# Relu-squared attention and a gated feed-forward product on one core: another order of the same 735 steps

## The chip, the cores and the metric

The kernel runs on one core of a Trainium2 chip. The metric is the time of one execution on the device in microseconds (us). Times are medians of several executions. A run that is more than 1.5% above the fastest of the same kernel counts as slow and is left out. The span in a profile is the time of the one execution that was profiled, and is about 2 us shorter than the time on the clock of the same run.

TensorE is called PE in the profile (its weight loads PEld), VectorE DVE, ScalarE ACT, GpSimd POOL, SyncE SP.

## The reference

```python
# q, k, v: (8 batches, 12 heads, 448 tokens, 64) float32
scores = np.matmul(q, k.transpose(0, 1, 3, 2)) / 8.0
attn   = np.maximum(scores, 0.0) ** 2 / 448
x      = np.matmul(attn, v).transpose(0, 2, 1, 3).reshape(3584, 768)
h      = x @ w_in                                  # w_in  (768, 2048)
g      = h * (1.0 / (1.0 + np.exp(-1.702 * h)))
out    = g @ w_out                                 # w_out (2048, 768), result float32
```

## The kernel before

The work is cut into 24 units (a batch by four heads). For each unit, the kernel loads q, k and v, brings q and k into transposed form, computes seven blocks of scores, relus, squares them, and multiplies by v. The first six units are loaded with a cast and transposed on TensorE; later ones are loaded by Sync, cast by ScalarE and GpSimd, and transposed by DMA. The token blocks of x are gathered in eight groups; each group passes through the two feed-forward products.

Nothing is scheduled by a tool: the order of all instructions is one list of short words that a loop reads. Each engine executes its instructions in the order of that list.

```python
        zp = ps_m.tile([128, 512], F32, name="zp", tag="mm")
        for _ in range(8):
            nc.tensor.matmul(out=zp, lhsT=zero[:, 0:128], rhs=zero[:, 0:512], start=True, stop=True)
        # ... cut ...
        def slot(how, u, j):                        # "s": one block of scores, then its relu
            sc = scores(u, j, 2 if "t" in how else 1)
            if "h" in how:                          # ":h": relu held until the next f step
                held.append((u, j, sc))
            else:
                ats[u, j] = relu2(u, j, sc, "d" in how)   # ":d": relu on VectorE, else ScalarE

        def zeros(how, n):                          # "z": n matmuls of zeros into a scores bank
            early.append(ps_s.tile([128, 2, 512], F32, name="sc", tag="sc"))
            for _ in range(n):
                nc.tensor.matmul(out=early[0][:, 0, :], lhsT=zero[:, 0:128],
                                 rhs=zero[:, 0:512], start=True, stop=True)

        do = {"s": slot, "x": square, "z": zeros,
              "k": lambda how, u: trans_pe(u, "k"), "q": lambda how, u: trans_pe(u, "q"),
              # ... cut: a, b attention x v; f first product; m, p, i second product ...
              "jk": lambda how, u: load16(u, "k"), "jq": lambda how, u: load16(u, "q"),
              "jv": lambda how, u: load_v(u), "jw": lambda how, i: w1(i),
              "jo": lambda how, h, i: w2(h, i), "I": lambda how: make_identity(nc, ident),
              # ... cut: G gate; L, W later loads; K, Q casts; R transposes by DMA ...
```

The zero matmuls compute nothing that is used: they only keep TensorE active while the first loads are on their way. The loads `jk`, `jq`, `jv` (of k, q, v), `jw` (w_in), `jo` (w_out) and the making of the identity `I` are all issued by GpSimd, in listed order. And the buffers of q and k have three places each, so a fourth `jq` has to wait until the first q was transposed.

## Time and profile before

| | before |
|---|---|
| median (lowest to highest) of 4 runs | 389.35 us (389.01 to 389.63) |
| span of the profiled execution | 388.4 us |
| TensorE busy | 370.6 us of it |
| lost on TensorE in the first 24 us | 8.8 us |
| lost later | 8.6 us, 2.4 of it on one wait for w_out |

The profiled execution was at the upper end (390.16 us on the clock), so that differences between traces come out up to 0.8 us smaller than those between medians.

The two lines below are from TensorE's instructions in order of time, before: start, duration, the operation and its tiles, and the count of instructions in the row.

```profile
4.61 1.16 PE L466 MATMUL sc<-zero 128*128 128x512 f16 x3
5.70 0.58 PE L129 MATMUL tr<-ident,q 128*64 128x128 f16 x14
```

The old order lists the step `z3` first. TensorE is active from 1.22 us until the first transpose at 5.70. The second view is of busy time in stretches (columns: stretch, its length, then busy time of PE, PEld, DVE, ACT, POOL with the number of instructions, the granted clock, the share of the DMA rings and GB/s).

```profile
5.30:8.70 3.40, 2.34 (x62) 1.43 (x60) 1.81 (x3) 0.37 (x1) 3.40 (x6) 1.00 1.21 178
8.70:12.10 3.40, 1.87 (x50) 1.38 (x50) 2.98 (x6) 2.27 (x3) 2.10 (x4) 1.00 1.20 180
```

TensorE waits for loads here, but it still works 2.34 and 1.87 of 3.40 us.

### The profile page before, as it was taken

Reading aid. Unit: us, or ns where it says so; the run is one execution under the profiler, and the core shown is the slowest. Engines: PE = TensorE matmul, PEld = TensorE weight load, DVE = VectorE, ACT = ScalarE, POOL = GpSimd, SP = SyncE. Lnnn points to the kernel's source line nnn. Section 1 sums busy time; section 2 is a strip of 40 time slices with the busy share of each in tenths; the row PEclk is TensorE's granted clock in tenths of the full one; section 3 lists DMA queues with packets and bytes.
Section 4 is the critical chain, followed back from the end, with each engine's and each line's share of the span. In section 5 each row is a group of like instructions: output and inputs, shape, how many; then the busy total and the mean of one; then the engine's idle time right before and its main releaser. Section 6 shows DMA issues by size and latency. Waiting matters only on the chain.

```text
span 388.4 us, 8391 instructions
## 1 busy us (share of the span) xinstructions
PE 370.6 (95%) x3390; PEld 195.4 (50%) x3390; DVE 262.4 (68%) x433; ACT 218.4 (56%) x320; POOL 136.8 (35%) x200
## 2 busy tenths in 40 slices
PE   7699999799999999999999999999999999999994
PEld 3566654344444545454455455555455555545552
DVE  3889774689977987846767777377965845114474
ACT  2796855578748546566865948446934452242210
POOL 8537417516443213344451244212234132232100
PEclk9999999999999999999999999999999999999999
DMA  8999999999750769899774194643140600210323
GB/s 117 199 203 182 204 259 198 233 216 176 207 138 2 145 168 193 183 230 207 181 173 133 41 154 102 154 99 110 25 106 0 130 1 17 66 42 1 83 81 82
DMA packets 65223, 50.88 MB, mean 131 GB/s; under 512 B 35744, under 2 KB 61728, under 8 KB 65184
## 3 DMA queue, kind: packets, MB, share of 16 engines
q1 hardware_dynamic: 47872, 35.70, 37.7%
q0 software_dynamic: 17152, 14.55, 25.8%
q8 instruction: 26, 0.43, 0.4%
q10 hardware_dynamic: 160, 0.10, 0.1%
q14 instruction: 13, 0.11, 0.1%
HBM read 45.61 MB, written 11.01 MB: 146 GB/s over the span
## 4 chain that ended last, share of the span: by engine, by line
PE 79%; DVE 9%; DMA 6%; issue 3%; POOL 2%; ACT 1%; ACTq 0%; POOLq 0%
PE ht L245 34%; PE op L310 27%; PE sc L166 8%; PE av L197 6%; DVE at L453 4%; DMA wout<-in_moe_w_out_dram 4%; DMA v<-in_v_dram 2%; PE op L271 2%; DVE osb L321 2%; DVE rl L177 1%; PE tr L129 1%; PE avm L197 1%; DVE xt L220 1%; ACT rl L180 1%; POOL k L119 1%
## 5 line engine op out<-in xcount | busy, mean ns | idle before, releaser
L245 PE MATMUL ht<-xt,win 128*128 128x512 f16 (+2 forms) x768 | 157.9, 353 | 0.2 <-ACT ea L319 0.2
L252 POOL TENSOR_SCALAR gt<-gf 128x512 f16<-128x512 f32 (+2 forms) x128 | 82.6, 645 | 214.0 <-ACT gf L250 212.4
L180 ACT ACTIVATE rl<-sc 128x896 f16<-128x896 f32 x148 | 130.1, 922 | 45.3 <-PE sc L166 37.0
L453 DVE TENSOR_TENSOR at<-rl 128x896 f16<-128x896 f16 x168 | 109.1, 681 | 17.8 <-ACT rl L180 17.4
L250 ACT ACTIVATE gf<-ht 128x512 f32<-128x512 f32 (+2 forms) x128 | 69.7, 548 | 87.8 <-PE ht L245 75.2
L245 PEld LDWEIGHTS <-win 128*128 128x128 f16 x768 | 72.1, 98 | 74.0 <-issue 11.6
L310 PEld LDWEIGHTS <-gt 128*128 128x128 f16 x424 | 40.5, 98 | 31.1 <-issue 4.5
L166 PE MATMUL sc<-qT,kT 64*64 64x448 f16 (+4 forms) x816 | 48.2, 324 | 2.3 <-ACT rl L180 1.5
L310 PEld LDWEIGHTS <-as 128*128 128x128 f16 x320 | 30.4, 98 | 24.3 <-issue 3.6
L310 PE MATMUL op<-wout,as 128*128 128x384 f16 x224 | 40.4, 326 | 0.0
L310 PE MATMUL op<-wsum,gt 128*128 128x384 f16 x224 | 40.2, 326 | 0.0
L217 DVE CAST xt<-av 128x768 f16<-128x768 f32 (+5 forms) x34 | 24.1, 735 | 20.4 <-PE av L197 20.4
L321 DVE SCALAR_TENSOR_TENSOR osb<-op,osb 128x384 f32<-128x384 f32 (+1 forms) x49 | 25.7, 545 | 15.4 <-PE op L310 15.2
L310 PE MATMUL op<-wout,gt 128*128 128x384 f16 (+1 forms) x200 | 35.3, 320 | 0.8 <-DVE osb L321 0.8
L197 PE MATMUL av<-at,v 64*64 64x448 f16 (+3 forms) x668 | 33.1, 331 | 1.2 <-DVE at L453 0.6
L166 PEld LDWEIGHTS <-kT 64*64 64x64 f16 x816 | 19.2, 105 | 25.2 <-issue 18.2
L305 DVE TENSOR_TENSOR as<-gt 128x1024 f16<-128x1024 f16 x38 | 27.6, 752 | 3.4 <-POOL gt L252 3.4
L321 DVE SCALAR_TENSOR_TENSOR osb<-op,ea 128x384 f32<-128x384 f32 x24 | 13.2, 551 | 24.4 <-ACT eb L319 12.6
L197 PEld LDWEIGHTS <-v 64*64 64x64 f16 x816 | 21.5, 107 | 16.3 <-issue 7.0
L177 DVE TENSOR_SCALAR rl<-sc 128x896 f16<-128x896 f32 x20 | 21.7, 1086 | 6.5 <-PE sc L166 6.4
L104 POOL CAST q<-qst 128x896 f16<-128x896 f32 x18 | 17.8, 987 | 6.3 <-DMA qst<-in_q_dram 5.5
L91 POOL DMA_DIRECT2D v<-in_v_dram x24 | 18.1, 757 | 1.0
(38 smaller groups left out, 167.4 us busy)
## 6 DMA issues: line engine op xcount, KB each, us to landing
out_dram<-osb SPq DMA_DIRECT2D x54, 192.0 KB, 3.0
kst<-in_k_dram SPq DMA_DIRECT2D x18, 448.0 KB, 5.4
qst<-in_q_dram SPq DMA_DIRECT2D x18, 448.0 KB, 5.8
v<-in_v_dram POOLq DMA_DIRECT2D x24, 224.0 KB, 6.2
win<-in_moe_w_in_dram POOLq DMA_DIRECT2D x8, 384.0 KB, 9.5
wout<-in_moe_w_out_dram POOLq DMA_DIRECT2D x4, 768.0 KB, 12.5
q<-in_q_dram POOLq DMA_DIRECT2D x6, 224.0 KB, 7.4
k<-in_k_dram POOLq DMA_DIRECT2D x6, 224.0 KB, 8.6
```

The lines of the kernel that those rows point to most:

```text
L166: nc.tensor.matmul(out=sc[c, a, c0:c0 + 64 * (q1 - q0)], lhsT=st["kT"][r, kb, c], rhs=st["qT"][r, q0:q1, c], start=True, stop=True)
L177: nc.vector.tensor_scalar(out=rl, in0=sc[:, :, 0:S], scalar1=0.0, scalar2=None, op0=ALU.max)
L180: nc.scalar.activation(out=rl, in_=sc[:, :, 0:S], func=AF.Relu)
L197: nc.tensor.matmul(out=st["av"][s][64 * a:64 * a + 64, 64 * (q0 - base):64 * (q1 - base)], lhsT=st["v16"][r, a, 64 * kb:64 * kb + 64], rhs ...
L217: nc.vector.tensor_copy(out=xts[g][:, 2 * pr:2 * pr + 2, c], in_=st["pair"][:, :, f])
L245: nc.tensor.matmul(out=ht[:, 0:n], lhsT=w[:, kk, fo:fo + 128], rhs=xts[g][:, kk, 0:n], start=(kk == 0), stop=(kk == NK - 1))
L250: nc.scalar.activation(out=gf[:, 0:n], in_=ht[:, 0:n], func=AF.Gelu_apprx_sigmoid, scale=1.0 / SC)
L252: nc.gpsimd.tensor_scalar(out=gts[g][:, f, 0:n], in0=gf[:, 0:n], scalar1=SC, scalar2=1.0, op0=ALU.mult, op1=ALU.mult)
L305: nc.vector.tensor_tensor(out=out_, in0=x, in1=y, op=op)
L310: nc.tensor.matmul(out=op[:, 0:cw], lhsT=lhs[:, f, :], rhs=w[:, f, c0:c0 + cw], start=(start and f == 0), stop=(stop and f == HF - 1))
L321: nc.vector.scalar_tensor_tensor(out=o, in0=op[:, 0:w], scalar=sc, in1=add, op0=ALU.mult, op1=ALU.add)
L453: nc.vector.tensor_tensor(out=at, in0=rl, in1=rl, op=ALU.mult)
```

## The change

The list of words is replaced by another one. The multiset of steps is the same but for the marks `:d`, `:h` and `:m`. The new list is meant to share the DMA rings better between the engines that issue transfers, and to place loads, casts and transposes of batch 2 and later well ahead of their use. It also gives VectorE 31 relus in place of 20. The core of the diff, with cuts:

```diff
         words = (
-            "z3 jq0 jk0 I jk1 q0 jq2 k0 s0.0:d x0.0 jq1 s0.1 jk2 s0.2 q2 x0.1 jv1 k1 jv0 s0.3 "
+            "jk0 I k0 jq0 q0 s0.0 jk1 s0.1 s0.2:d k1 jq1 x0.0 jk2 z3 q1 jq2 k2 s1.0 x0.1 jq5 "
 # ... cut ...
-            "s5.2 x5.1 s5.3 a4:m s5.4 x5.2 x5.3 x5.4 s5.5 s5.6:d x5.6 K6 K7 x5.5 m0.1.0 a5 "
-            "m0.0.0 f1.0 jo1.1 jo1.0 f1.1 f1.2 Q7 R6 f1.3 s6.0 L8 C1 s6.1:d K8 R7 C3 x6.1 Q8 W6 "
+            "s4.5 x4.3 x4.5 x4.4 s4.6 f0.12 f0.13 x4.6 s5.0 s5.1 x5.0 a4 jo1.0 s5.2:h f0.14 "
+            "f0.15 s5.3 x5.1 s5.4:d x5.2 s5.5 x5.3 x5.4 s5.6 x5.5 L7 C0 m0.1.0 x5.6 K6 Q6 R6 Q7 "
+            "C2 a5 jo1.1 m0.0.0 f1.0 L8 f1.1 f1.2 C3 C1 f1.3 f1.4 f1.5 s6.0 s6.1:d s6.2 x6.0 "
+            "x6.1 K7 f1.6 x6.2 s6.3 s6.4:d R7 x6.3 E2 B3 f1.7 f1.8 K8 Q8 f1.9 f1.10 W6 R8 s6.5 "
 # ... cut: all later lines are re-ordered in the same way ...
```

## The prediction

> **What bounds the kernel now.** I read the page first (busy shares, chain), then PE's waits, then PE's instructions in order of time, then busy time in 10 us stretches.
>
> ```profile
> PE 370.6 (95%) x3390; PEld 195.4 (50%) x3390; DVE 262.4 (68%) x433; ACT 218.4 (56%) x320; POOL 136.8 (35%) x200
> PEclk9999999999999999999999999999999999999999
> ...
> PE 79%; DVE 9%; DMA 6%; issue 3%; POOL 2%; ACT 1%; ACTq 0%; POOLq 0%
> ```
>
> TensorE is the bound: 370.6 of 388.4 us busy at full clock, 79% of the chain. So a new order can only gain what PE waits. Where that is:
>
> ```profile
> 7.70 0.78 PE L166 MATMUL sc<-qT,kT 64*64 64x256 f16 x32 [0.72 <-DVE kT L133]
> 9.21 0.58 PE L129 MATMUL tr<-ident,q 128*64 128x128 f16 x14 [0.74 <-DMA q<-in_q_dram]
> 11.29 0.58 PE L129 MATMUL tr<-ident,q 128*64 128x128 f16 x14 [0.79 <-DMA q<-in_q_dram]
> 12.38 0.58 PE L129 MATMUL tr<-ident,k 128*64 128x128 f16 x14 [0.51 <-DMA k<-in_k_dram]
> 14.30 0.39 PE L166 MATMUL sc<-qT,kT 64*64 64x256 f16 x8 [0.63 <-ACT rl L180]
> 15.19 0.97 PE L197 MATMUL avm<-at,v 64*64 64x256 f16 x40 [0.50 <-DMA v<-in_v_dram]
> 18.61 0.39 PE L197 MATMUL avm<-at,v 64*64 64x192 f16 x8 [0.68 <-DVE at L453]
> ...
> 75.45 2.77 PE L271 MATMUL op<-wout,gt 128*128 128x384 f16 x16 [2.43 <-DMA wout<-in_moe_w_out_dram]
> ```
>
> The start waits for loads, then for relu on ACT and squares on DVE; at 75 us the first right-half output product waits 2.43 us for a wout quarter. The stretches, columns PE, PEld, DVE, ACT, POOL busy, show who is full then:
>
> ```profile
> 10.00:20.00 10.00, 6.59 (x236) 5.07 (x231) 8.31 (x17) 7.63 (x10) 5.38 (x8) 1.00 1.24 199
> 20.00:30.00 10.00, 9.36 (x233) 6.34 (x227) 8.82 (x18) 9.10 (x14) 3.32 (x6) 1.00 1.25 202
> 200.00:210.00 10.00, 10.00 (x94) 5.46 (x93) 7.27 (x11) 5.08 (x9) 1.92 (x4) 1.00 0.88 230
> ```
>
> From 100 us on nearly every stretch has PE at 10.00: nothing to win there. DVE is the full engine at the start.
>
> Matmul ends are modelled, so "busy" hides short waits. I therefore laid PE's listed work end to end by start-to-start spacings of the trace (24 matmuls of 512 columns in 5.18 us, 8 of 384 in 1.30, a score or attention step of four tiled matmuls 0.19, 14 transposes 0.43, 0.095 at each change between tiled and full-array work) and subtracted this "work position" from the real start. The lag is 8.8 us at 24 us, 11.2 at 55, 13.9 at 75, 15.8 at 98, 16.6 at 139 and 17.4 at 380. The remaining 5 us are the last evacuation and store. So 17.4 us is the whole purse: half is spent in the first 24 us, 2.6 on the wout quarter, and about 1.6 after 100 us.
>
> **What the Trainium skill says.** "DMA: Bandwidth & Descriptors", section "Issuing engines are not separate DMA queues": transfers of all issuing engines run on the same 16 DMA engines and interleave. The trace agrees: while both late wout quarters were in flight (landing 8.5 and 13.7 us after issue), a transpose issued at 65.0 us took 10.3 us, against 2.9 at the least. "TensorE: Matmul & The Clock Gate", section "Back-to-back issue gap": N/2.4 + 2.5 ns for N columns when warm; the trace has 215.8 ns for 512, so PE has no slack inside a product. Same page, section on the HAM clock gate: about 3.4 us of activity before full speed; here the zero matmuls start 427 ns apart for the first ten. "Perfetto Trace Analysis", section "Tensor Engine Instruction": the reported end is an estimate, hence my use of start times.
>
> **The change, part by part.** The set of steps is the same: 3390 matmuls in both, 135 changes between array modes in both, so PE's work is equal (my positions end at 365.2 us for both). Eleven more relus go to DVE (31 for 20): 11 x 1.09 = 12 us more DVE, about 10 us less ACT, spread out. What moves:
>
> (a) The start. k of unit 0 is loaded first and q third on Pool after making the identity; three zero matmuls move behind the first scores. By hand, with the trace's durations (relu 0.87 ACT or 1.09 DVE, square 0.57, transpose copy 0.62, landings of the old first loads 5.2, 8.0, 9.2, 11.3, 12.3 us): k lands 5.2, q about 6.9 (it was 6.35 for the second load), first score 8.2 instead of 7.7; unit 1's scores 12.05 against 12.9; then DVE is busy without a break from 9 us. The new order wants 15 squares, two DVE relus and 6 copies before the third attention step, where the old had about 12 squares and one relu before its first f step. That gives f0.0 at 27.3 us, position 16.8, lag 10.5, where the old order has 8.8 at that position. Unit 3's first score then waits for a k copy queued on DVE to 29.1: lag 11.6. So **+2 to +3 us** lost. My chain is on the pessimistic side, since I gave DVE strict listed order and no luck; I book +2.
>
> (b) 24 to 60 us: the old order loses 2.4. The new one has done more scores by then and has fewer left; I book 1.5, so **-0.9**. Its loads of the first wout half are issued in the other order, after all qkv of batches 0 and 1, so the gate on the Sync queue opens near 51 us instead of 46; unit 6's loads land near 56.5 (54.2 before), and its transposes near 62, still 5 us before its scores (position 54.7 + lag 12.5 = 67). The first output product at 52.4 needs a quarter landing near 51: no wait, thinly.
>
> (c) The right-half wout quarters: one is issued at position 37.6 instead of 48, the other at 44.1, but behind two casts on Pool that wait for unit 7's load (about 60.3 us). So only one quarter, not two, is in flight after 60 us: it should land at 67 to 70. The product that needs it stands at position 63, about 75 us. The 2.6 us wait goes: **-2.6**.
>
> (d) Unit 6's v: issued at position 62.5 instead of 52.3 (Pool), after two f steps, used at 69.3. That is 6.8 us of PE work less about 1.5 until Pool gets there, against a load of median 6.2 us that shares the rings with unit 9's loads and unit 8's transposes. I book **+0.8**, 0 to 2.5.
>
> (e) Later loads: the listed lead from transpose to first score becomes 8.1 us or more for every unit from 6 on (the old listing has 1.3 and 1.8 for units 6 and 11, though Sync runs ahead of it). A pair of transposes takes about 6 us. The old trace shows hardly a wait on those after 100 us, so this buys almost nothing: **-0.3**. The waits at 96 to 98 us (1.6, DVE relu and squares) and 134 to 139 us (0.8) may shrink: **-0.3**, held down by the added DVE relus.
>
> Sum: +2 - 0.9 - 2.6 + 0.8 - 0.3 - 0.3 = -1.3; with 389.4 us before, 388.1. As (a) is the pessimistic term and the order was presumably chosen because it did well in its author's tool, I lean by another half microsecond: **387.5 us**.
>
> **The rivals.** First, the start is no worse, or better: if DVE's squares and copies pack better than by hand, (a) is 0 or -1, and the result is 384 to 385. For it: earlier unit 1 scores and zero matmuls placed where PE waits anyway. Against it: DVE already 83 to 88% busy there and more asked of it. Second, a new DMA wait replaces the old: unit 6's v, or the two Pool casts stuck on unit 7's load, holding f1's scaling on Pool and through three gf buffers PE; +2 to +4 us, 390 to 392. For it: the transfers are at their limit to about 60 us and Pool is in order. Against it: PE reaches f1 near 59 us and has three buffers of grace. Third, DVE becomes the bound between 80 and 140 us: 31 relus there in place of 20; old stretches already show it at 9.5 and 10.0 of 10 us (90 to 100 and 130 to 140). That would be +1 to +3. Fourth, the clock: only eight zero matmuls (3.4 us) come before the first idle, so PE may run its first transposes at half speed, costing up to 0.5 us. Fifth, the extra lead is hidden anyway and everything cancels: about 389.
>
> **Range and chances.** The terms are independent with errors of about 2 (start), 1 (v), 1 (DVE), 1 (24 to 60 us): some 2.7 together. Range **383.5 to 391.5**. Faster by 2% needs below 381.6, that is 7.8 of the 17.4 us lag gone: the whole middle plus part of the start; chance **0.07**. Slower by 2% needs 397.2: **0.03**. Within 2%: **0.90**.
>
> **What would show it.** Right: PE busy within 1 us of 370.6; first score near 8.2 us; f0.0's first matmul between 25 and 28 us; no PE wait on wout over 0.5 us; first wait on a v load near 80 us at most 2.5 us; DVE busy up by about 12 us and ACT down by about 10; hardly a PE wait after 140 us. Wrong: f0.0 near 22 us or PE waits in the first 30 us summing to less than in the old trace (then (a) has the wrong sign), PE waiting for transposes of units 6 to 11, or waits on DVE of several us between 80 and 140 us.

## The result, and the profile after

| | before | after |
|---|---|---|
| median (lowest to highest), 4 runs each | 389.35 us (389.01 to 389.63) | 393.28 us (391.95 to 394.72) |
| span of the profiled execution | 388.4 us | 391.5 us |
| TensorE busy | 370.6 us | 371.6 us |

The ratio is 1.0102 (95% interval 1.0066 to 1.0139). Ratios in this document are the mean time of one kernel's fast runs over that of the other's of the same rounds, so not quite the ratio of the medians. The result is correct. The kernel is 1% slower: within the 2% called "the same", but outside the predicted range.

The page of the kernel after, its busy times and its chain of waits:

```profile
PE 371.6 (95%) x3390; PEld 197.4 (50%) x3390; DVE 268.0 (68%) x441; ACT 209.1 (53%) x309; POOL 133.6 (34%) x200
PE 78%; DMA 8%; DVE 4%; issue 3%; ACT 3%; POOL 2%; SPq 1%; ACTq 0%; POOLq 0%
```

Against before, VectorE's share of the chain fell from 9 to 4% and that of the DMA rose from 6 to 8%: on the chain, waits moved from relus and squares to loads. TensorE's instructions in order of time, after, at the places that the prediction was about:

```profile
1.22 3.60 PE L428 MATMUL zp<-zero 128*128 128x512 f16 x8 [1.22 <-DVE zero L425]
5.35 0.96 PE L129 MATMUL tr<-ident,k 128*64 128x128 f16 x14 [0.53 <-DMA k<-in_k_dram]
7.95 0.96 PE L129 MATMUL tr<-ident,q 128*64 128x128 f16 x14 [1.64 <-DMA q<-in_q_dram]
9.63 1.33 PE L166 MATMUL sc<-qT,kT 64*64 64x256 f16 x32 [0.72 <-DVE qT L133]
10.89 0.96 PE L129 MATMUL tr<-ident,k 128*64 128x128 f16 x14
11.79 1.46 PE L466 MATMUL sc<-zero 128*128 128x512 f16 x3
...
24.51 0.81 PE L466 MATMUL sc<-zero 128*128 128x512 f16 x3 [1.16 <-ACT rl L180]
...
71.31 1.46 PE L245 MATMUL ht<-xt,win 128*128 128x512 f16 x6 [0.53 <-ACT gf L250]
...
81.08 2.77 PE L271 MATMUL op<-wout,gt 128*128 128x384 f16 x16
...
89.21 1.52 PE L197 MATMUL av<-at,v 64*64 64x448 f16 x28 [1.64 <-DMA v<-in_v_dram]
```

Read the durations, not only the waits. The three zero matmuls at 11.79 us last 1.46 us, the same three at 24.51 last 0.81. The transposes last 0.96 us, where those of the old kernel last 0.58; the first 32 score matmuls 1.33 against 0.78. TensorE ran at half clock until nearly 14 us. In the old kernel only the zero matmuls did.

The page's row of granted clock does not tell: it shows full speed in every slice before, and in all but the last after, and the mean clock is 0.999 before and 0.997 after. The trace's own clock record explains it: the record begins with the first change (at 5.31 us before, at 13.80 us after), and what lies ahead of it is counted as full. The spacing of equal matmuls has to be looked at: starts of 512-column matmuls are 427 ns apart at half clock and 216 at full in these traces.

The stretches after, cut at the clock's own steps (same columns as before; the 1.00 of the clock column is wrong in these three, for the reason just given):

```profile
3.60:7.00 3.40, 2.17 (x17) 0.87 (x15) 0.62 (x1) 0.00 (x0) 2.67 (x4) 1.00 1.05 139
7.00:10.40 3.40, 1.73 (x38) 1.61 (x42) 0.62 (x1) 0.14 (x1) 1.18 (x2) 1.00 1.22 186
10.40:13.80 3.40, 3.40 (x49) 1.89 (x42) 2.15 (x3) 1.59 (x2) 1.69 (x3) 1.00 1.23 191
```

TensorE was busy 64% and 51% of the first two stretches and stayed slow; it was busy in all of the third, and the clock came up at its end.

Where did the time go? The same lag as in the prediction (real start of a step less its position when TensorE's work is laid end to end at full clock), worked out from the two traces, in us:

```
position of the step:   9     12     25     44     62     72     86    126    end
before                3.64   5.67   9.77  11.23  13.90  14.01  15.81  16.60  17.37
after                 6.11   9.02  15.09  17.29  18.03  19.95  20.19  20.25  20.51
difference            2.47   3.35   5.32   6.06   4.13   5.94   4.38   3.65   3.14
```

The start costs 6.1 us to position 44. From 44 to 62 the new order gains 1.9 back: the wait for w_out is gone (the product at 81.08 has none), less 0.7 lost around 71.31, where TensorE waits for a gf buffer (gf is a tile of the first product after its activation on ScalarE, until GpSimd has scaled it). From 62 to 72 it loses 1.8 on the v load of unit 6. After that it gains 2.8, since the old order loses 3.4 us there and the new one 0.6. The sum is 3.1 us, as the spans say.

### The profile page after: what moved, and what is told of

It reads as the page before. It is cut to its first block, busy times and chain, and to the rows that moved or that the text cites. A ratio compares the mean times of both kernels' runs of the same rounds, so it can differ in the third digit from the quotient of the medians.

```text
span 391.5 us, 8379 instructions
## 1 busy us (share of the span) xinstructions
PE 371.6 (95%) x3390; PEld 197.4 (50%) x3390; DVE 268.0 (68%) x441; ACT 209.1 (53%) x309; POOL 133.6 (34%) x200
## 4 chain that ended last, share of the span: by engine, by line
PE 78%; DMA 8%; DVE 4%; issue 3%; ACT 3%; POOL 2%; SPq 1%; ACTq 0%; POOLq 0%
PE ht L245 33%; PE op L310 29%; PE sc L166 8%; PE av L197 7%; DMA wout<-in_moe_w_out_dram 3%; DMA qst<-in_q_dram 2%; ACT rl L180 2%; DMA v<-in_v_dram 2%; DMA q<-in_q_dram 1%; DVE osb L321 1%; DVE at L453 1%; POOL gt L252 1%; PE tr L129 1%; ACT gf L250 1%; POOL q L104 1%
## 5 line engine op out<-in xcount | busy, mean ns | idle before, releaser
L252 POOL TENSOR_SCALAR gt<-gf 128x512 f16<-128x512 f32 (+2 forms) x128 | 79.9, 624 | 211.6 <-ACT gf L250 209.3
L180 ACT ACTIVATE rl<-sc 128x896 f16<-128x896 f32 x137 | 120.4, 918 | 46.6 <-PE sc L166 42.6
L453 DVE TENSOR_TENSOR at<-rl 128x896 f16<-128x896 f16 x168 | 105.6, 657 | 13.8 <-ACT rl L180 13.0
L245 PEld LDWEIGHTS <-win 128*128 128x128 f16 x768 | 72.3, 98 | 73.8 <-issue 11.2
L166 PE MATMUL sc<-qT,kT 64*64 64x448 f16 (+4 forms) x816 | 49.5, 328 | 5.5 <-DVE qT L133 1.9
L177 DVE TENSOR_SCALAR rl<-sc 128x896 f16<-128x896 f32 x31 | 33.6, 1087 | 16.5 <-PE sc L166 15.9
L197 PE MATMUL av<-at,v 64*64 64x448 f16 (+4 forms) x736 | 35.6, 326 | 2.9 <-DMA v<-in_v_dram 1.6
L217 DVE CAST xt<-av 128x768 f16<-128x768 f32 (+6 forms) x37 | 26.0, 728 | 12.4 <-PE av L197 12.3
L305 DVE TENSOR_TENSOR as<-gt 128x1024 f16<-128x1024 f16 x38 | 25.4, 695 | 3.3 <-POOL gt L252 3.3
L104 POOL CAST q<-qst 128x896 f16<-128x896 f32 x18 | 17.4, 964 | 11.5 <-DMA qst<-in_q_dram 10.6
L102 ACT ACTIVATE k<-kst 128x896 f16<-128x896 f32 x18 | 17.0, 949 | 5.4 <-DMA kst<-in_k_dram 5.4
```

What stands on the lines that cost most here:

```text
L166: nc.tensor.matmul(out=sc[c, a, c0:c0 + 64 * (q1 - q0)], lhsT=st["kT"][r, kb, c], rhs=st["qT"][r, q0:q1, c], start=True, stop=True)
L177: nc.vector.tensor_scalar(out=rl, in0=sc[:, :, 0:S], scalar1=0.0, scalar2=None, op0=ALU.max)
L180: nc.scalar.activation(out=rl, in_=sc[:, :, 0:S], func=AF.Relu)
L197: nc.tensor.matmul(out=st["av"][s][64 * a:64 * a + 64, 64 * (q0 - base):64 * (q1 - base)], lhsT=st["v16"][r, a, 64 * kb:64 * kb + 64], rhs ...
L217: nc.vector.tensor_copy(out=xts[g][:, 2 * pr:2 * pr + 2, c], in_=st["pair"][:, :, f])
L245: nc.tensor.matmul(out=ht[:, 0:n], lhsT=w[:, kk, fo:fo + 128], rhs=xts[g][:, kk, 0:n], start=(kk == 0), stop=(kk == NK - 1))
```

## The experiments

Every kernel below gave the correct result. "Warm" and "cold" stand for full and half clock. Times are medians of four runs beside runs of the kernel before on the same chip (389.27, 389.17, 389.11 and 389.35 us in the four batches, of seven runs each with one slow one of 434.51 left out), except where one look is said. The theories were: the start is slow because the clock stays low (clock); because q of unit 0 comes late behind k and the identity (load); because VectorE is full (VectorE, the prediction's own); and, for the late part, that v of unit 6 is issued too late. The gains of e1, e2, e3 and e6 all came out larger than their expectations said.

Each kernel has one trace but four runs, and the clock's course is not the same in all runs of one kernel. The mean clocks show it for the kernel before: its 15 fast runs with a mean clock of 0.997 or more took 388.61 to 389.58 us (median 389.08), the 12 with 0.996 or less 388.88 to 390.53 (median 389.90). So what a trace says of the clock holds for that run, and tenths of a microsecond between medians of four are not worth much.

**Joining the halves (e4_old_start and e5_new_start).** All steps that both lists have up to `m0.0.0` stand in the order of one list, those after it in the order of the other; the few that only one list has in its first part follow just behind `m0.0.0` (in e4_old_start, the two right-half w_out quarters among them).

```diff
 e4_old_start
-  jk0 I k0 jq0 q0 s0.0 jk1 ...  (new order)  ... m0.0.0   | new order after it
+  z3 jq0 jk0 I jk1 q0 jq2 k0 ... (old order) ... m0.0.0   | new order after it
 e5_new_start
+  jk0 I k0 jq0 q0 s0.0 jk1 ...  (new order)  ... m0.0.0   | old order after it
```

> The new order, but every step up to and including the second output product of group 0 stands in the old order, so the old start is joined to the new rest. In the profile of the new kernel TensorE's lag behind its own listed work is 17.3 us at that point against 11.2 in the old one, and after it grows by 3.2 us against 6.2. Theory 'two parts': the start loses 6.1 us and the rest gains 3.0, independently; then this kernel takes 389.35 - 3.0 = 386.4 us (385.6 to 387.2). Rival 'lateness': the rest gains only because TensorE comes 6 us late, which gives the loads that much more time; then the waits come back and it takes 388.5 to 390.

Measured: 386.97 us (386.92 to 387.45), ratio 0.9939 (0.9925 to 0.9954), span 384.8.

> The mirror: new start up to the second output product, old order after it. 'Two parts': 393.3 + 3.0 = 396.3 us (395.3 to 397.3). 'Lateness': the late start gives the old rest its slack, no wait on the right-half wout quarters, and it takes about 393 (392.3 to 394).

Measured: 393.89 us (three fast runs, 393.47 to 395.88; a slow one of 401.24 left out), ratio 1.0135 (1.0094 to 1.0175).

So the new start alone costs 4.5 us (393.89 less 389.35; 5.3 by the ratio of the means) and the new rest alone gains 2.4 (389.35 less 386.97). Together they would make +2.1 to +2.9, and +3.9 was measured, so the halves are not quite independent. e4_old_start came out as 'two parts' said. e5_new_start missed that range and lies in the rival's: from `m0.0.0` on, its old rest loses 1.5 us less than in the kernel before, so part of those waits is hidden by lateness. Two single lines show what belongs to which half. In e4_old_start the wait for w_out is gone and that for v has come; in e5_new_start it is the w_out wait that is there, shorter than before (1.22 for 2.43 us) because TensorE arrives later. TensorE's instructions in e4_old_start, then in e5_new_start:

```profile
74.54 2.77 PE L271 MATMUL op<-wout,gt 128*128 128x384 f16 x16
82.56 1.52 PE L197 MATMUL av<-at,v 64*64 64x448 f16 x28 [1.54 <-DMA v<-in_v_dram]
```

```profile
79.52 2.77 PE L271 MATMUL op<-wout,gt 128*128 128x384 f16 x16 [1.22 <-DMA wout<-in_moe_w_out_dram]
```

**The zero matmuls back in front (e1_zeros_first), and q second as well (e3_zeros_q).**

```diff
 e1_zeros_first
-  jk0 I k0 jq0 q0 ... jk2 z3 q1
+  z3 jk0 I k0 jq0 q0 ... jk2 q1
 e3_zeros_q
+  z3 jk0 jq0 I k0 q0 ... jk2 q1
```

> The new order with the three zero matmuls moved back to the front, as the old order has them. Theory 'clock': the new start lets TensorE go idle after 3.4 us of activity, so its first transposes took 0.96 us instead of 0.58 and the first scores 1.33 instead of 0.78; with the zeros in front the clock is up at 5.5 us, those durations fall back to 0.58 and 0.78, the lag at the first score falls from 3.9 to about 3.3 and the time by 1 us or more, to 391.5 to 392.5. Rival 'loads and VectorE set the pace anyway': durations fall but the time stays at 393 to 393.8.

Measured: 390.36 us (389.31 to 391.38), ratio 1.0023 (0.9997 to 1.0050), 2.9 us under the new kernel.

> The same and also unit 0's q load issued second, before the identity is made, as early as in the old order. q should land near 6.4 us instead of 7.9 and the first score start near 7.7 instead of 9.6. Theory 'late first loads': about 2 us of the 3.4 us of extra lag at the first ff step go, so 391.0 to 391.8. Rival 'VectorE is full': the scores come earlier but the first ff step stays near 28 us because squares, copies and VectorE relus are in the way; then 392.5 to 393.5.

Measured: 388.39 us (387.90 to 388.96), ratio 0.9974 (0.9958 to 0.9989). With both, the new order's start is mended by 4.9 us. In the trace of e1_zeros_first the clock record shows full speed from 5.49 us, but half speed again from 12.31 to 15.73, so that this run does not measure the whole worth of a warm start.

**More zero matmuls, order untouched (e6_more_zeros).** This is the test of the clock alone: not one word of the list is moved.

```diff
-        for _ in range(8):
+        for _ in range(12):
             nc.tensor.matmul(out=zp, lhsT=zero[:, 0:128], rhs=zero[:, 0:512], start=True, stop=True)
```

> The new order untouched, but 12 zero matmuls instead of 8 ahead of everything; the three later zero matmuls stay where the new order has them. It separates the clock from the place of the three. Theory 'clock': the trace's clock record starts full speed at about 5.3 us instead of 13.8, unit 0's transposes take 0.58 us instead of 0.96, and the time falls by 1.5 to 2.5 us to 390.8 to 391.8. Rival 'the three zeros stand in the path': nothing is gained, 393 to 394, as four more zeros even hold back the first transpose by 0.5 us.

Measured: 389.69 us (389.16 to 390.00), ratio 1.0010 (0.9993 to 1.0027). Four matmuls that compute nothing take 3.6 us off the new kernel. The transposes of e6_more_zeros:

```profile
6.13 0.58 PE L129 MATMUL tr<-ident,k 128*64 128x128 f16 x14
7.37 0.58 PE L129 MATMUL tr<-ident,q 128*64 128x128 f16 x14 [0.66 <-DMA q<-in_q_dram]
```

They run at full clock. q is also a little earlier: its transposes start at 7.37 and not at 7.95, though the load was issued in the same place. So this kernel does not hold the load strictly fixed.

**q second, zeros untouched (e2_q_second), and the same with a cold clock (e8_q_second_cold).**

```diff
 e2_q_second
-  jk0 I k0 jq0 q0 s0.0
+  jk0 jq0 I k0 q0 s0.0
 e8_q_second_cold: the same, and
-        for _ in range(8):
+        for _ in range(4):
```

> The new order with only unit 0's q load issued second, before the identity is made; the clock stays late. If the late q and the late clock are separate costs, the first score starts about 1.3 us earlier and the time is 393.3 - 1.5 = 391.8 (391.0 to 392.5). If the slow clock and VectorE hide it, 393 to 393.8.

Measured: 388.85 us (387.84 to 389.74), ratio 0.9981 (0.9959 to 1.0003). That is 4.4 us under the new kernel, far more than an earlier q was thought to give. The trace says why: the clock came up by itself, at 5.92 us. TensorE's instructions in e2_q_second:

```profile
5.14 0.94 PE L129 MATMUL tr<-ident,k 128*64 128x128 f16 x14 [0.33 <-DMA k<-in_k_dram]
6.25 0.58 PE L129 MATMUL tr<-ident,q 128*64 128x128 f16 x14 [0.18 <-DMA q<-in_q_dram]
7.56 0.78 PE L166 MATMUL sc<-qT,kT 64*64 64x256 f16 x32 [0.72 <-DVE qT L133]
```

The wait between the two transposes fell from 1.64 to 0.18 us, and the second one is already fast. But the early q did not raise the clock, which rose at 5.92, before q's transposes began. It rose at the end of a stretch that the zero matmuls and k's transposes had filled to 90%. In the trace of the new kernel the clock's stretches lay otherwise and cut the same eight zero matmuls in two, into 68% and 64%. Stretches of 3.41 us, the first of the new kernel, then two of e2_q_second:

```profile
0.14:3.55 3.41, 2.33 (x6) 0.89 (x7) 0.33 (x2) 1.49 (x2) 2.44 (x9) 1.00 0.14 8
```

```profile
2.51:5.92 3.41, 3.08 (x20) 1.28 (x18) 0.00 (x0) 0.00 (x0) 3.33 (x7) 1.00 1.01 142
5.92:9.33 3.41, 2.40 (x66) 1.81 (x63) 2.19 (x3) 1.34 (x2) 2.53 (x5) 1.00 1.19 178
```

Where these stretches lie differs from run to run, so whether the clock rises on eight zero matmuls is luck: with the new start it did in the traces of e2_q_second, a9_again and e10_filler, and did not in those of the new kernel and e5_new_start. What the earlier q did is to fill the stretch that followed (70% busy), and the clock stayed up. So load and clock are tied together, and the pair was repeated with the clock held down:

> The new order with q loaded second, but only 4 zero matmuls at the front instead of 8, so that TensorE idles from 3 to 5 us and the clock should come late although q is early. With q second and 8 zeros it was 388.85. Theory 'the slow clock is the cost, the early q only brought the clock up': 391.5 to 393.5, clock record starting after 8 us, first transposes 0.94 us. Rival 'the early q itself is the gain': 388.3 to 389.8.

Measured: 390.26 us (389.75 to 391.65), ratio 1.0028 (0.9997 to 1.0058); full clock from 11.51 us. It lies between what the two theories said.

**The old kernel with its zero matmuls later (b1_zeros_late), and cold (b2_cold).**

```diff
 b1_zeros_late (old list)
-  z3 jq0 jk0 I jk1 q0 jq2 k0 s0.0:d x0.0 jq1 s0.1 jk2 s0.2
+  jq0 jk0 I jk1 q0 jq2 k0 s0.0:d x0.0 jq1 s0.1 jk2 z3 s0.2
 b2_cold: the same, and
-        for _ in range(8):
+        for _ in range(4):
```

> The old order with one edit: its first three zero matmuls move behind the second load of k (between unit 0's second and third score), as in the new order. 'Clock': no full speed at 5.3 us; it comes at 10 us or later, the first transposes take 0.96 us, and the old kernel becomes 2 to 3 us slower, 391.2 to 392.3. Rival 'only the new order's start suffers': 389 to 390.

Measured: 390.00 us (389.51 to 390.69), ratio 1.0020 (1.0000 to 1.0040). The clock still came up at 5.49 us, after a stretch that was 91% busy without `z3`, and the old order's loads then came close enough together to hold it. So the place of `z3` is not needed to explain a warm start in this trace; as where the stretches lie is luck, one trace does not show that it never matters.

> The old order with 4 zero matmuls instead of 8 at the front and its three later ones moved behind the second k load: the old kernel made cold. With 8 it was 390.0 and the clock still came at 5.5 us. 'Clock': full speed after 8 us, 391.5 to 393.5. Rival 'a late clock costs only the new order': 389.5 to 390.5.

Measured: 390.94 us (390.31 to 392.24), ratio 1.0044 (1.0007 to 1.0080); full clock only from 12.76 us. A cold start costs the old order 1.8 us (390.94 less 389.11, the before of its batch), or 0.9 us over b1_zeros_late: at most half of what a warm start gives the new order. It lies between the two expected ranges.

**VectorE relieved (e9_no_dve_relu).** With twelve zero matmuls as in e6_more_zeros, both VectorE relus of the first two lines go back to ScalarE.

```diff
-  s0.2:d ... s2.1:d
+  s0.2   ... s2.1
```

> The new order with 12 zero matmuls in front (389.69) and the two relus that it gives VectorE in the start (0.2 and 2.1) put back on ScalarE. Theory of the prediction, 'VectorE is full in the start': VectorE has 2.2 us less to do, the first feed-forward step starts 1 to 2 us earlier and the time falls to 388.2 to 388.9. Rival 'ScalarE is as full': no gain or worse, 389.5 to 390.8.

Measured: 390.34 us (389.62 to 392.58), ratio 1.0034 (0.9995 to 1.0072), against 389.69 for e6_more_zeros. Nothing was gained. Stretches from 20 to 30 us, first of e6_more_zeros, then of e9_no_dve_relu:

```profile
20.00:30.00 10.00, 7.98 (x197) 5.80 (x189) 8.63 (x17) 7.32 (x10) 2.47 (x4) 0.83 1.24 202
```

```profile
20.00:30.00 10.00, 7.43 (x220) 5.03 (x208) 8.73 (x17) 9.05 (x12) 2.23 (x5) 1.00 1.21 195
```

VectorE did not become emptier (8.73 after 8.63 us), and ScalarE became fuller (9.05 after 7.32). The two stretches are not quite alike: that of e6_more_zeros holds a cold stretch from 22.80 to 26.21 us (its clock is 0.83). The two engines are about equally loaded, so the run speaks against VectorE alone as the bound of the start, and not against both together. The profiled run is also the slowest of the four, with a cold stretch from 9.33 to 12.74 us and a stall of 1.71 us at 31.24. But the two runs with mean clocks of 0.998 and 0.999 took 389.62 and 390.07 us, no less than e6_more_zeros.

**The new kernel once more (a9_again), one look.**

> The new kernel once more, unchanged, for a second look at its start. If the late clock belongs to this order and not to one unlucky run, the clock record starts after 8 us again and the first transposes take 0.9 us or more; otherwise about 5.5 us and a time near 390.

Measured: 391.45 us in a single run, as neither expectation said. The clock in it was up early, from 4.38 us, and went down again at 7.79 for two steps (and once more from 24.86 to 28.27). The stretches, cut at those steps:

```profile
4.40:7.80 3.40, 1.02 (x21) 0.59 (x22) 0.62 (x1) 0.00 (x0) 1.87 (x3) 1.00 1.00 138
7.80:11.20 3.40, 2.68 (x60) 2.31 (x56) 1.26 (x2) 1.38 (x2) 2.42 (x4) 0.50 1.26 198
11.20:14.60 3.40, 3.40 (x40) 1.98 (x40) 2.26 (x5) 0.35 (x1) 1.05 (x2) 0.50 1.23 194
```

TensorE is busy 30% of the first stretch, and the clock falls at its end. It is busy 79% of the second: not enough to raise it. It is busy in all of the third, and at 14.62 full speed returns. The same hole, the wait for q of unit 0, has the same effect by another way. No single wait in this stretch was longer than 1.90 us.

**Filling the hole (e10_filler).** Four zero matmuls are put between the first two transposes, where TensorE waits for q. They change neither the order of the loads nor when TensorE is free for q.

```diff
-  jk0 I k0 jq0 q0 s0.0
+  jk0 I k0 z4 jq0 q0 s0.0
```

> The new order with four more zero matmuls between unit 0's k transposes and its q transposes, where TensorE waited 1.64 us for the q load anyway; nothing else is touched, k is not held back and q stays late. In the 14 traces so far the clock went to full speed only after a stretch of 3.41 us with TensorE busy for 0.90 of it or more, and fell after one with 0.54 or less. Theory 'clock alone': the first 8 us now hold such a busy stretch, full speed comes before 8 us and holds through the first scores, and the time is 389.3 to 390.8. Rival 'late q, in itself, is the larger part' (the cold kernel with an early q took 390.26, which lies between the two theories): 391.5 to 393.5 although the clock is up.

Measured: 389.54 us (389.14, 389.49, 389.58 and 391.67), ratio 1.0021 (0.9982 to 1.0060). TensorE's instructions and two stretches of it:

```profile
5.21 0.58 PE L129 MATMUL tr<-ident,k 128*64 128x128 f16 x14 [0.73 <-DMA k<-in_k_dram]
5.73 1.04 PE L466 MATMUL sc<-zero 128*128 128x512 f16 x4
7.46 0.58 PE L129 MATMUL tr<-ident,q 128*64 128x128 f16 x14 [0.69 <-DMA q<-in_q_dram]
8.76 0.78 PE L166 MATMUL sc<-qT,kT 64*64 64x256 f16 x32 [0.72 <-DVE qT L133]
```

```profile
4.00:7.40 3.40, 2.04 (x20) 0.73 (x18) 0.62 (x1) 0.00 (x0) 2.27 (x4) 1.00 1.06 141
7.40:10.80 3.40, 2.51 (x63) 1.81 (x63) 1.84 (x3) 1.61 (x2) 2.46 (x4) 1.00 1.25 198
```

The clock came up at 4.02 us, before the four matmuls ran, and stayed: 60% busy held it, where 30% in a9_again did not. As it had come up in a9_again at nearly the same time (4.38), this pair of traces shows the hole alone. The wait at q is filled, and the gain of 3.7 us is the same as that of e6_more_zeros. As there, q came somewhat earlier than in the first profile of the new kernel (7.46 us for 7.95; a9_again, which is the new kernel itself, had 7.63), so a few tenths of the gain may be the load's.

Nor is all of the 3.6 to 3.7 us shown to be the clock's. Unit 1's first score starts at 14.76 us in the new kernel, at 12.24 in e6_more_zeros and at 12.33 in e10_filler. Of these 2.4 to 2.5 us, 0.5 to 0.6 are there already when q's transposes start, so the slow stretch itself costs some 2 us, an estimate from these starts. The other 1.1 to 1.2 us come after 30 us, with two stalls of TensorE in the new kernel's trace that nothing in it releases: 0.37 us at 38.18 (e10_filler has one of 0.40, e6_more_zeros none), and this one:

```profile
32.26 0.52 PE L197 MATMUL av<-at,v 64*64 64x192 f16 x17 [1.18 <-issue]
```

a9_again has no such stall. It stays 2.2 us behind e6_more_zeros from unit 1's first score to `f1.0`, and took 1.8 to 1.9 us more than the medians of the two warm kernels. Whether the stalls have to do with the clock is not shown.

**The better version (e7_v6_early).** e4_old_start still waits 1.54 us for v of unit 6. Its load is moved ahead by five f steps and five score steps:

```diff
-  f1.5 s6.0 s6.1:d ... f1.9 f1.10 W6 R8 s6.5
+  f1.5 W6 s6.0 s6.1:d ... f1.9 f1.10 R8 s6.5
```

> The joined kernel (old start, new rest) with unit 6's v load issued five feed-forward steps earlier on Pool, right after step f1.5. The wait of 1.73 us of attention step 6 for that v should go and the time fall from 387.0 to 385.2 (384.8 to 385.7). Rival: the v load now shares the rings with the right-half wout quarters, which land later, and a wait on wout comes back; then 386.5 to 388.

Measured: 386.48 us (385.47 to 386.79), ratio 0.9924 (0.9904 to 0.9944). It is the fastest of all kernels here, 2.9 us (0.8%) under the kernel before. The wait for v is gone from TensorE's waits, and none on w_out came back. The gain over e4_old_start is only 0.5 us of the 1.5 that went, within the spread of the runs and less than was expected: the profiled run lost 1.5 us elsewhere in the start (lag 10.09 against 8.62 at position 17), where its clock record has a half-speed stretch from 22.8 to 26.2 us. The other runs agree with that: three had a mean clock of 0.990 to 0.992 and took 386.32 to 386.79 us, the fourth had 0.996 and took 385.47, as expected. In e4_old_start it was 0.997 to 0.999.

Two by two, the start of the new order in medians:

| | profiled run cold to 11.5 or 13.8 us | profiled run warm from 4.0 to 5.9 us |
|---|---|---|
| q of unit 0 after the identity | 393.28 (after) | 389.69 (e6_more_zeros), 389.54 (e10_filler) |
| q of unit 0 second | 390.26 (e8_q_second_cold) | 388.85 (e2_q_second) |

The warm column gains 3.6 to 3.7 us with the late q, and 1.4 with the early one. An early q gives 3.0 us cold and 0.7 to 0.8 warm; e1_zeros_first and e3_zeros_q are a second warm pair and give 2.0. The two do not add up, since both act on the same early stretch. The columns go by the profiled runs alone, and "warm" is not warm throughout: e6_more_zeros was at half clock again from 22.80 to 26.21 us and e2_q_second from 16.16 to 19.58.

## Why the prediction was wrong

The prediction said 387.5 us with a range to 391.5; 393.28 came. Its main reading stands: TensorE is the bound, its work is unchanged (371.6 us busy for 370.6), and only waits and lag moved. Its own checks, step by step:

- **(a) The start, +2 us booked.** The sign was right, the size and the reason were not. With (b), +1.1 was booked to position 44 and +6.1 came. The first score started at 9.63 us (said: near 8.2), unit 1's first score at 14.76 (said: 12.05), f0.0 at 28.90 (said: 25 to 28). The failing step is the clock: the hand chain of (a) took its durations from the old trace, where the transposes and scores ran at full clock, and half speed is reckoned only in the sentence on the fourth rival: "so PE may run its first transposes at half speed, costing up to 0.5 us". The mechanism named was the right one, and its size was not: keeping the clock up, by e6_more_zeros or e10_filler, gives 3.6 to 3.7 us in medians, seven times the 0.5, and some 2 us, four times, if only the slow stretch itself is counted. What was reckoned was the first transposes at half speed. In fact the whole stretch to 13.80 us ran so: the eight zero matmuls were cut in two by the clock's stretches, and the wait of 1.64 us for q left the next one 51% busy.
- **What else the start cost.** Worked out on the same positions, e10_filler and e6_more_zeros have a lag of 13.7 at position 44, where the old order has 11.2. So 2.4 to 2.5 us are left with a warm clock, against the 1.1 booked. "DVE is full" was given as the reason. e9_no_dve_relu speaks against VectorE alone: taking two relus off it gained nothing. The count behind it was also of unlike points: before the third attention step the old list has 13 squares and the new one 15, before f0.0 16 and 18, so only two more are asked of VectorE, not 15 against 12. Part is q, which landed at 7.91 us instead of 6.9, and 7.3 to 7.4 in the warm runs; moving it up gains 0.7 to 0.8 us of the warm time.
- **(c) w_out, -2.6 us.** Right: no wait at the product at 81.08 us. The quarters landed at 64.15 and 78.06 us; the one needed there is the first. That it was "only one quarter in flight" is not shown, since e4_old_start, with the quarters issued at 54.06 and 55.01 us, landed its second at 71.11 and had no wait either. The earlier issue may be enough.
- **(d) v of unit 6, +0.8 (0 to 2.5).** In its range: 1.64 us of wait, 1.8 to 1.9 of lag. Together with the gf wait this is the second rival, which came true. Before TensorE's wait at 71.31, GpSimd stood idle 9.10 and 1.51 us before two casts of q (at 65.68 and 68.14), waiting for their loads; its scalings began only at 70.02, and ScalarE waited 1.77 us for them. The two parts cost 2.5 us of lag (said: 2 to 4).
- **(e) and the waits after 80 us, -0.6.** Too small: the gain after position 72 was 2.8 us. The old order's late waits on relus and squares are gone. e5_new_start, with the old rest, still has them (two waits of 0.52 and 0.57 us near 100 us, with the same two lengths at 96 to 98 us in the kernel before). The third rival, VectorE as the bound from 80 to 140 us, falls with that; it rested on a misreading, since 31 and 20 are the relus of the whole kernel, and between 80 and 140 us VectorE has 5 in either trace.
- **The engines.** ScalarE's busy time fell by 9.3 us (said: about 10). VectorE's rose by 5.6, not 12: its relus cost what was said (11.9 us), but a square got cheaper, 657 ns for 681 in the mean or 3.5 us in all, and the sums of line L305 took 25.4 us for 27.6.
- **Hardly a TensorE wait after 140 us:** right, one of 0.45 us near the end.

Put together, in lag: booked -1.3. The cold start adds 3.6 (clock, q and the stalls after 30 us), the rest of the start 1.3, the gf wait 0.7, v 1.0 more than booked, and the late part takes off 2.2 more than booked: +3.1, which is what the spans differ by. The extra half microsecond, taken off because "the order was presumably chosen because it did well", had no measurement behind it and went the wrong way.

What stays open: how much of the 2.4 us in the warm start is the order of the loads and how much the order of scores and squares; and what the stalls after 30 us are. That the old start with the new rest loses less after position 44 (2.4 us) than the new kernel (3.2) is mostly the gf wait (0.7): in e4_old_start GpSimd's casts began at 53.18 and 55.97 us, ahead of its first scaling for f1, and TensorE has no wait on gf.

## What to carry to other kernels

At a start that waits for loads, look at how densely TensorE is used in every stretch of some 3.4 us, and not only at the longest wait: waits of 0.5 to 1.9 us that follow each other kept the clock at half or brought it back there, and four matmuls of zeros in the hole took 3.7 us off. Eight zero matmuls in front (3.6 us) raised the clock in some traces and not in others; with eleven (before) or twelve (e6_more_zeros) a whole stretch of 3.41 us was 100% busy. Order the first loads so that the two operands of the first product come right behind each other, ahead of anything else that the issuing engine has to make. When a new order is better in one part and worse in another, cut the two lists at a common step and join them: each half is then measured, and the join was better than either.

## What the Trainium skill lacked or had wrong

- "TensorE: Matmul & The Clock Gate", section "What's actually happening": it gives a free-running window of 3413 ns, a cold start, full speed after a busy window and half after an idle one. The traces agree with the window: the half-speed stretches that begin and end inside a trace last 3.41 or 6.83 us (9.33 to 12.74, 7.79 to 14.62). What lacks is how busy is busy: the section "A second HAM failure mode: psum-queue depth-cycling" has short idles bring the clock down, but gives no share. In the traces here the clock rose only after windows in which TensorE was busy at least 82% of the time (e10_filler; 90% and more in the others), did not rise at 79% or less, fell after windows of 54% or less, and held from about there up. These shares come from modelled ends of matmuls, and the phase of the window differs from run to run.
- The same page, section "Why this matters for your kernels": "No PE-idle gaps >~3µs". Here the longest gap was 1.90 us (a9_again) and the clock fell.
- The section first named puts the warm-up penalty under 1% of a typical kernel span and says not to fit to a count of cold matmuls. Here a warm start took 3.6 of 393 us off, 0.9%: in line with the figure, and yet about as much as lies between the two tuned orders (3.9).
- The same page, section "Part 4: PE-mode transpose", says that full speed does not engage for transposes. Fourteen transposes took 0.96 us cold and 0.58 warm, so they do run faster at the full clock. They also seem to count as activity: the clock rose after 2.51 to 5.92 us of e2_q_second, where zero matmuls alone fill 67%, and not after 0.14 to 3.55 us of the new kernel, where they fill 68%.
- "Runtime: NRT & Kernel Launch", section "Instruction fetch mechanics", has instructions refilled in blocks of 16 KiB and calls the cost mostly hidden; it gives no size for a late one. In the traces here TensorE has stalls inside a group of matmuls that nothing in the trace releases. There is one of 1.18 us that ends at 32.26 us in the kernel after, and one of 0.67 us that ends at 32.45 in the kernel before. Each ends 2.4 us after a 16 KB read on the instruction queue began (at 29.82 and at 30.07 us). The same holds, with 2.3 to 2.6 us, for those of 0.50 to 1.71 us in e4_old_start, e9_no_dve_relu, b1_zeros_late and b2_cold. That it is the fetching of instructions is an inference, not tested.
